# Half a batch of attention outputs turned on TensorE instead of by transposing transfers, with the order of commands written anew

## The chip, the cores and the metric

The kernel runs on one core of a Trainium2 chip. The metric is device time in microseconds (us) of one execution; the time of a version is the median over its runs. The profile is of one execution, and its span runs from that execution's first instruction to its last.

## What is computed

Masked attention over 4 batches of 8 heads (768 rows, 64 columns a head) is followed by a feed-forward layer that takes the largest of three products. "Retrieval" heads see every earlier row, the others only 4 sink rows and a window of 64.

```python
scores = scale * np.matmul(q, k.transpose(0, 1, 3, 2))
mask = np.where(retr[0, :, 0, 0, None, None], full_mask, stream_mask)
scores = np.where(mask[None, :, :, :], scores, -1000000000.0)
a = np.exp(scores - np.max(scores, axis=-1, keepdims=True))
a = a / (np.sum(a, axis=-1, keepdims=True) + 1e-09)
attn = np.matmul(a, v)                        # (4, 8, 768, 64)
x = attn.transpose(0, 2, 1, 3).reshape(4 * 768, 512)
h = np.maximum(np.maximum(x @ w1, x @ w2), x @ w3)   # (3072, 768)
out = h @ w_out                               # (3072, 512)
```

## The kernel before

The work is cut into batches (0 to 3) and halves of 384 rows. The order of all instructions is written out by hand: `PROGRAM` is a tuple of strings of short commands, and the loop at lines 843 to 846 calls a function for each, which issues its instructions there and then. Each engine works through its own in that order and waits where a tile isn't ready; so the table sets the order on every engine and on every queue of transfers. The commands that matter here, with their arguments (b batch, half, hp pair of heads):

- `load b quad` (line 248) loads keys and queries (tile kq) from POOL's queue, with a cast to 16 bits; `turn` (line 264) transposes them in 32 x 32 blocks on DVE into KQ. Batch 0 has its own path (`hl`, `cast`, `turnp`, `s0`, `k0`, `kx0`): two-head loads, casts, transposes on TensorE.
- `load_v b half s` (line 290) loads values from SP's queue in three transfers; `v` and `y` (lines 476, 512) cast them into the tiles va and vx. The last letter of a command names the engine that does it: d DVE, a ACT, p POOL, r DVE by a reduction. There are three buffers for the loaded values.
- `w 0` to `w 3` (line 391) load the three weights of the layer (w0t, w1t, w2t) and the output weight (woutt) from POOL's queue. `gs` (line 283) is a transfer of 4 bytes out of a weight tile on SP's queue: SP waits there until that weight has landed, and what follows on SP's queue comes later.
- `s b unit` (line 639) is a unit of scores on TensorE, followed by its exponentials on ACT (line 691) into tiles pt; there are two score tiles (st) in PSUM. `k` (line 696) multiplies pt by a mask, on POOL or DVE. `kx` gathers keys that the masks pick.
- `av b half hp` (line 703) multiplies probabilities with values for a pair of heads and divides by the sums on DVE (lines 722, 724). The result x has rows on the partitions and must be transposed into xT. With a trailing `D`, a transposing transfer on SP's queue does it (line 730). Without it, `x b half hp e` (line 736) does it: three TensorE transposes into a PSUM bank, then a copy by engine e (line 743).
- `f b half wi ni` (line 434) is one of 18 products of a half: four matmuls of 384 columns, then on ACT or DVE a cast (wi = 0) or on DVE a maximum (wi = 1, 2) into acc and hT. `o b half tb` (line 454) is an output block: six matmuls with woutt, a copy and a store on SP's queue.
- `idle n` (line 321) issues n matmuls on zeros, whose result nothing reads.

All TensorE results but the scores share four PSUM banks. In the table before, batch 0's half 0 is turned by TensorE, and in its half 1 pairs 0, 1 and 2 go by transfer and pair 3 by TensorE. All later halves go by transfer.

Of the kernel before, what the change touches and what calls it, by code (L numbers as in the profile page):

```python
# [96 lines left out]
    "s0 1 1 2, y 0 1 4:5:1 r r, gs 0, k0 0 3 2 d, f 0 0 0 5 a, kx 1 0 a, k0 2 1 0 p, turn 1 0 1 0",
    "k0 3 0 2 p, av 0 1 0 D, av 0 1 1 D, f 0 0 0 4 a, turn 1 1 0 0, turn 1 1 0 1, f 0 0 0 2 a",
    "f 0 0 0 0 a, f 0 0 1 0, load 2 0, f 0 0 1 5, turn 1 1 1 1, s0 1 2 2, k0 2 0 1 p",
    "turn 1 1 1 0, f 0 0 1 3, f 0 0 1 2, k0 2 0 0 p, y 0 1 5:8:2 r a, f 0 0 1 1, k0 3 1 2 p",  # L100
    "f 0 0 1 4, s 1 0, av 0 1 2 D, kx 1 1 p, k0 2 1 1 p, k0 2 3 1 p, av 0 1 3, f 0 0 2 0",
    "f 0 0 2 1, s 1 1, f 0 0 2 5, k 1 0 X 1 d, k 1 1 Y 0 p, f 0 0 2 2, turn 2 0 0 0, f 0 0 2 4",
    "turn 2 0 1 0, x 0 1 3 a, s 1 2, f 0 0 2 3, f 0 1 0 5 a, f 0 1 0 3 a, k 1 1 X 1 p",
    "turn 2 0 1 1, f 0 1 0 1 d, s 1 7, k 1 2 X 0 p, f 0 1 0 2 d, flags, load_v 1 0 s, v 1 0 0 d",
    "y 1 0 1:8:2 s a, v 1 0 1 a, gs 0, k 1 2 Y 0 d, y 1 0 4:5:1 s r, k 1 0 Y 0 p, f 0 1 0 0 d",
    "w 3, v 1 0 2 d, f 0 1 1 2, s 1 3, f 0 1 2 2, f 0 1 1 1, load_v 1 1 s, k 1 3 Y 0 p, f 0 1 1 3",
    "f 0 1 2 3, y 1 0 4:5:1 r a, y 1 0 1:8:2 r a, gs 0, f 0 1 0 4 d, s 1 5, k 1 0 X 0 d",
    "k 1 1 X 0 p, load_v 2 0 s, y 2 0 1:8:2 s a, f 0 1 1 5, f 0 1 2 5, y 1 1 1:8:2 r r",
    "k 1 7 X 1 p, y 1 1 4:5:1 r r, f 0 1 1 4, k 1 5 X 1 p, av 1 0 0 D, s 1 6, load 2 1",
    "av 1 0 1 D, v 1 1 2 d, f 0 1 1 0, v 1 0 3 a, f 0 1 2 0, f 0 1 2 1, k 1 2 X 1 p, av 1 0 2 D",  # L110
    "av 1 0 3 D, s 1 4, k 1 4 X 1 p, k 1 4 Y 0 p, f 0 1 2 4, v 1 1 3 p, o 0 0 0 a, o 0 0 1 a",
    "k 1 3 X 1 p, o 0 1 1 a, k 1 7 Y 1 d, turn 2 1 0 1, turn 2 1 1 1, k 1 4 X 0 p, v 1 1 1 p",
    "turn 2 1 0 0, turn 2 0 0 1, v 1 1 0 p, load_v 3 0 s, v 2 0 0 a, o 0 0 2 a, guess",
    "turn 2 1 1 0, f 1 0 0 1 a, f 1 0 0 0 a, f 1 0 1 0, f 1 0 0 5 d, k 1 7 X 0 p, v 2 0 1 p",
    "f 1 0 0 4 d, s 2 0, k 1 3 X 0 p, f 1 0 2 0, k 1 7 Y 0 d, load 3 0, k 1 6 X 0 p, f 1 0 1 4",
    "k 1 5 Y 0 d, v 2 0 2 a, kx 2 0 d, kx 2 1 a, f 1 0 2 4, f 1 0 1 1, k 1 5 X 0 d, f 1 0 0 3 a",
    "f 1 0 1 5, f 1 0 1 3, k 1 6 Y 0 p, av 1 1 3 D, av 1 1 1 D, s 2 1, k 2 1 Y 0 p, av 1 1 0 D",
    "y 2 0 1:8:2 r a, f 1 0 2 3, k 2 0 Y 0 p, gp 1 2, f 1 0 2 1, y 2 0 4:5:1 s a, av 1 1 2 D",
    "k 2 1 X 0 p, y 2 0 4:5:1 r a, v 3 0 0 p, s 2 4, f 1 0 2 5, f 1 0 0 2 d, load 3 1",
    "y 3 0 4:5:1 r d, v 2 0 3 a, f 1 0 1 2, f 1 0 2 2, s 2 2, k 2 2 X 0 d, f 1 1 0 0 d",  # L120
    "k 2 1 X 1 p, k 2 0 X 1 p, f 1 1 0 4 a, f 1 1 1 0, y 3 0 1:8:2 s a, k 2 2 X 1 d, turn 3 0 0 0",
    "y 3 0 1:8:2 r p, f 1 1 0 5 d, load_v 3 1 s, s 2 7, f 1 1 0 2 d, k 2 0 X 0 p, f 1 1 0 1 a",
    "o 0 1 0 d, f 1 1 1 1, av 2 0 0 D, k 2 4 Y 0 d, f 1 1 1 2, f 1 1 1 5, load_v 2 1 s",
    "k 2 4 X 1 d, k 2 7 Y 1 d, f 1 1 1 4, k 2 7 X 0 d, o 1 0 2 d, s 2 3, k 2 3 X 1 p",
    "turn 3 0 1 0, gs 0, k 2 2 Y 0 d, f 1 1 0 3 a, o 0 1 2 a, av 2 0 1 D, s 2 6, y 2 1 1:8:2 r a",
    "f 1 1 2 0, k 2 6 X 0 p, av 2 0 3 D, f 1 1 1 3, k 2 7 Y 0 d, s 2 5, k 2 6 Y 0 d, av 2 0 2 D",
    "f 1 1 2 4, f 1 1 2 3, f 1 1 2 5, turn 3 1 0 1, k 2 3 X 0 p, y 3 0 4:5:1 s a, o 1 0 1 a",
    "k 2 5 X 1 p, turn 3 0 1 1, turn 3 1 1 1, k 2 3 Y 0 p, v 3 1 0 d, v 2 1 2 a, o 1 0 0 a",
    "k 2 7 X 1 p, f 1 1 2 2, f 2 0 0 0 a, f 1 1 2 1, f 2 0 1 0, k 2 4 X 0 d, f 2 0 2 0",
    "f 2 0 0 1 a, turn 3 1 1 0, f 2 0 0 2 d, f 2 0 1 2, y 2 1 4:5:1 r p, v 3 0 3 p, v 3 1 2 a",  # L130
    "v 2 1 0 a, turn 3 1 0 0, f 2 0 0 4 a, f 2 0 1 4, v 3 1 1 p, turn 3 0 0 1, v 2 1 1 p",
    "kx 3 0 d, f 2 0 0 3 d, y 3 1 1:8:2 r d, k 2 5 Y 0 d, f 2 0 1 3, f 2 0 2 3, o 1 1 0 a, s 3 1",
# [909 lines left out]
```

## Time and profile before

| what | value |
|---|---|
| median of 3 runs | 190.68 us |
| all runs | 189.65, 190.68, 196.97 us |
| span of the profiled execution | 195.2 us |
| TensorE (PE) busy | 180.9 us, 93% of the span |
| DVE, ACT, POOL busy | 145.0, 98.8, 81.8 us |
| mean granted TensorE clock | 0.983 |

The profile gives the profiled execution's span and no other time of its own; the span lies 4.5 us above the median and 1.8 us below the slowest run. PE is TensorE's matmuls, DVE is VectorE, ACT is ScalarE, POOL is GpSimd, SP is the engine that only issues transfers; a q behind an engine's name (SPq) is its queue. L437 is line 437 of the kernel before. A row of a timeline gives start, duration, engine, line, what was written and read, and a count, with idle time and what ended it in brackets. A row of the windows gives, for a stretch of the span, each engine's busy time with its instructions, then the granted clock, the share of time that the transfer engines were busy (over 1 where packets wait) and GB/s.

### The profile page before, as it was taken

To read this page: it belongs to the slowest core of one execution; us is meant where nothing else is said; L and a number is where in the kernel's file an instruction comes from. 1 tells how busy PE (TensorE), PEld (TensorE's weight loads), DVE (VectorE), ACT (ScalarE), POOL (GpSimd) and SP (SyncE) were. 2 spreads that over 40 slices of the span, in tenths; PEclk is the share of its full clock that TensorE was granted. 3 is DMA by queue.
4 is the path that set the end of the run, shared out by engine and by line. 5 is a ranking of instruction groups with operands and counts; after the bars stand their busy time and mean duration, and the time that the engine had idled before them with its cause. 6 is when DMAs were issued, how large, how long until landed. Compare 5 with 4: busy or idle time off the path is not lost.

```text
span 195.2 us, 4739 instructions
## 1 busy us (share of the span) xinstructions
PE 180.9 (93%) x1854; PEld 106.1 (54%) x1854; DVE 145.0 (74%) x308; ACT 98.8 (51%) x158; POOL 81.8 (42%) x140
## 2 busy tenths in 40 slices
PE   7896899998994899999999999999999999999990
PEld 2443646664562445675556565755665566565550
DVE  3758999987997393879897989857794689465541
ACT  3598797377944534679529532775434400211110
POOL 7595978819682296039705600332612500000000
PEclk9999999999999589999999999999999999999999
DMA  5999999999999647935969310241033012401413
GB/s 177 329 325 267 207 213 207 116 164 189 160 187 227 97 133 158 242 99 108 210 167 241 93 58 0 77 114 57 0 66 129 0 57 59 134 0 54 161 54 116
DMA packets 44248, 26.59 MB, mean 136 GB/s; under 512 B 31038, under 2 KB 39742, under 8 KB 44222
## 3 DMA queue, kind: packets, MB, share of 16 engines
q1 hardware_dynamic: 38798, 17.54, 36.8%
q0 software_dynamic: 4192, 7.87, 23.8%
q10 hardware_dynamic: 1232, 0.85, 1.4%
q8 instruction: 15, 0.25, 0.5%
q14 instruction: 11, 0.09, 0.1%
HBM read 25.17 MB, written 6.29 MB: 161 GB/s over the span
## 4 chain that ended last, share of the span: by engine, by line
PE 66%; DMA 12%; DVE 11%; SPq 5%; issue 2%; ACT 1%; ACTq 0%; DVEq 0%
PE yy L437 34%; PE yy L462 15%; DMA vs<-in_v_dram 8%; PE oacc L717 6%; PE st L674 5%; DMA qs<-in_q_dram 4%; SPq L302 4%; DVE KQ L272 4%; PE yst L437 3%; DVE x L724 2%; DVE acc L449 1%; PE yst L462 1%; DVE KQ L241 1%; SPq L283 1%; DVE vx L800 1%
## 5 line engine op out<-in xcount | busy, mean ns | idle before, releaser
L377 POOL TENSOR_TENSOR pt<-pt,kb 128x512 f16<-128x512 f16 (+5 forms) x53 | 48.3, 931 | 67.4 <-ACT pt L691 55.5
L691 ACT ACTIVATE pt<-st 128x1024 f16<-128x1024 f32 (+2 forms) x51 | 43.5, 908 | 24.6 <-PE st L674 24.2
L437 PE MATMUL yy<-xT,w2t 128*128 128x384 f16 x184 | 36.8, 330 | 0.0
L437 PE MATMUL yy<-xT,w0t 128*128 128x384 f16 x180 | 34.9, 326 | 0.6 <-DMA xT<-x 0.6
L437 PE MATMUL yy<-xT,w1t 128*128 128x384 f16 x176 | 34.4, 326 | 0.1
L462 PE MATMUL yy<-woutt,hT 128*128 128x512 f16 (+1 forms) x138 | 32.8, 384 | 0.0
L449 DVE TENSOR_TENSOR hT<-yy,acc 128x384 f16<-128x384 f32 x46 | 25.2, 555 | 6.8 <-PE yy L437 5.1
L449 DVE TENSOR_TENSOR acc<-yy,acc 128x384 f16<-128x384 f32 x44 | 24.0, 555 | 7.9 <-PE yy L437 4.0
L272 DVE STREAM_TRANSPOSE KQ<-kq 128x384 f32<-128x384 f32 x24 | 25.4, 1134 | 0.4 <-DMA kq<-in_q_dram 0.4
L437 PEld LDWEIGHTS <-w0t 128*128 128x128 f16 x192 | 18.1, 98 | 13.5 <-issue 1.7
L445 ACT CAST acc<-yy 128x384 f16<-128x384 f32 x27 | 12.9, 489 | 23.3 <-PE yy L437 21.2
L437 PEld LDWEIGHTS <-w1t 128*128 128x128 f16 x192 | 17.9, 98 | 12.3 <-issue 1.0
L437 PEld LDWEIGHTS <-w2t 128*128 128x128 f16 x192 | 17.8, 98 | 12.3 <-issue 0.9
L462 PEld LDWEIGHTS <-hT 128*128 128x128 f16 x150 | 14.8, 101 | 16.5 <-issue 2.0
L717 PE MATMUL oacc<-va,pt 128*128 128x65 f16 x392 | 19.1, 195 | 4.4 <-ACT va L478 3.5
L717 PEld LDWEIGHTS <-pt 128*128 128x128 f16 x472 | 17.6, 98 | 8.3 <-issue 4.4
L471 ACT COPY ot<-yy 128x512 f32<-128x512 f32 (+1 forms) x14 | 7.9, 566 | 23.6 <-PE yy L462 20.9
L724 DVE TENSOR_TENSOR x<-oacc,sums 128x384 f16<-128x384 f32 x32 | 17.8, 557 | 1.1
L629 ACT ACTIVATE pt<-st 128x1024 f16<-128x1024 f32 (+5 forms) x22 | 15.5, 760 | 3.1 <-PE st L608 2.9
L674 PE MATMUL st<-KQ 32*128 32x128 f16 (+2 forms) x342 | 15.3, 263 | 0.0
L377 DVE TENSOR_TENSOR pt<-pt,kb 128x256 f16<-128x256 f16 (+4 forms) x31 | 11.7, 383 | 1.8 <-ACT pt L691 1.7
L445 DVE CAST acc<-yy 128x384 f16<-128x384 f32 x18 | 10.0, 557 | 3.8 <-PE yy L437 3.3
(117 smaller groups left out, 187.6 us busy)
## 6 DMA issues: line engine op xcount, KB each, us to landing
out_dram<-ot SPq DMA_DIRECT2D x23, 256.0 KB, 2.2
vs<-in_v_dram SPq DMA_DIRECT2D x18, 256.0 KB, 6.0
ks<-in_k_dram SPq DMA_DIRECT2D x8, 192.0 KB, 5.1
kq<-in_k_dram POOLq DMA_DIRECT2D x3, 384.0 KB, 8.1
kq<-in_q_dram POOLq DMA_DIRECT2D x3, 384.0 KB, 9.2
kq<-in_k_dram POOLq DMA_DIRECT2D x3, 288.0 KB, 7.9
kq<-in_q_dram POOLq DMA_DIRECT2D x3, 288.0 KB, 10.0
qs<-in_q_dram ACTq DMA_DIRECT2D x4, 192.0 KB, 4.8
```

Of the source, the lines that this page charges most:

```text
L272: nc.vector.transpose(out=dst.rearrange("c (p j) -> c j p", j=n)[:, j0:j1], in_=src.rearrange("c (j i) -> c j i", i=R),)
L377: engine.tensor_tensor(out=x, in0=x, in1=of_blocks(kb, pattern, rows), op=ALU.mult)
L437: nc.tensor.matmul(yy[:, 0:HALF], w_t[wi][:, ks, ni * P : (ni + 1) * P], xT[b, half, ks].rearrange("p a t -> p (a t)"), start=(ks == 0), s ...
L445: op(out=acc[b, half, ni], in_=yy[:, 0:HALF])
L449: nc.vector.tensor_tensor(out=acc[b, half, ni] if wi == 1 else hT[b, half, ni], in0=yy[:, 0:HALF], in1=acc[b, half, ni], op=ALU.max,)
L462: nc.tensor.matmul(yo[:, 0:n], hT[b, half, ns][:, tb * P : (tb + 1) * P], woutt[:, ns, c : c + n], start=(ns == 0), stop=(ns == NNB - 1),)
L471: op(out=ot[:, c : c + n], in_=yo[:, 0:n])
L629: nc.scalar.activation(out=pts[0, half, hp, u][:, r0:r1, c0:c1], in_=sts[hp][:, r0:r1, c0:c1], func=AF.Exp, scale=sc,)
L674: nc.tensor.matmul(sts["XY"[g // 2]][:, g % 2, c0 : c0 + n * P], KQ[rows, 0, ki * P : (ki + 1) * P] if kind == "p" else kx[b % 2][quad][ro ...
L691: nc.scalar.activation(out=pts[b, s, xy][:, r0:r1, c0:c1], in_=st[:, r0:r1, c0:c1], func=AF.Exp, scale=sc,)
L717: nc.tensor.matmul(o[:, i, r, 0 : D + 1], at[b, h, kind, ki, qi], vv[:, 0 : D + 1], start=(n == 0), stop=(n == len(todo) - 1), skip_group_ ...
L724: nc.vector.tensor_tensor(out=x, in0=o[:, :, :, 0:D], in1=rc.unsqueeze(3).to_broadcast([P, HB, 2, D]), op=ALU.mult,)
```

## The change

Only `PROGRAM` differs. `av 0 1 0`, `av 0 1 1` and `av 0 1 2` lose their `D`, and `x 0 1 0 d`, `x 0 1 1 a` and `x 0 1 2 a` are added; so three transfers go, and nine transposes, one copy on DVE and two on ACT come. Two of the `idle` commands are new with 2 matmuls each and one with 1: 18 such matmuls stand where 13 stood. Many other commands stand in another place, through the whole table, one goes to another engine (the cast of the queries of batch 0, half 1, pair 3, from DVE to POOL), and there are three more `gs 0`. Two of the places as lines of the table:

```diff
-    "s0 1 1 2, y 0 1 4:5:1 r r, gs 0, k0 0 3 2 d, f 0 0 0 5 a, kx 1 0 a, k0 2 1 0 p, turn 1 0 1 0",
-    "k0 3 0 2 p, av 0 1 0 D, av 0 1 1 D, f 0 0 0 4 a, turn 1 1 0 0, turn 1 1 0 1, f 0 0 0 2 a",
+    "av 0 1 0, av 0 1 1, f 0 0 0 5 a, w 2, k0 3 0 2 p, kx 1 0 a, k0 2 1 0 p, f 0 0 0 0 a",
+    "turn 1 0 1 0, turn 1 1 1 0, f 0 0 0 4 a, f 0 0 0 2 a, turn 1 1 0 1, turn 1 1 1 1",
+    "turn 1 1 0 0, x 0 1 1 a, s0 1 2 2, f 0 0 1 0, k0 3 1 2 p, k0 2 1 1 p, f 0 0 1 3",
```

Three places in the queues follow. Rows are instructions in an engine's order: line, operation, tile written <- tile read, shape, count. The lines of the changed kernel are four higher.

SP's queue, from the gate on w1t to the first transposing transfers of batch 1, before:

```order
L283 DMA gates<-w1t 1x2x1
L283 DMA gates<-w0t 1x2x1
L730 DMA_TRANSPOSE xT_685<-x 128x3x128
L730 DMA_TRANSPOSE xT_712<-x 128x3x128
L730 DMA_TRANSPOSE xT_828<-x 128x3x128
L302 DMA vs<-in_v_dram 128x8x64 x3
L283 DMA gates<-w0t 1x2x1
L302 DMA vs<-in_v_dram 128x8x64 x3
L283 DMA gates<-w0t 1x2x1
L302 DMA vs<-in_v_dram 128x8x64 x3
L730 DMA_TRANSPOSE xT_1207<-x 128x3x128
```

and now:

```order
L287 DMA gates<-w1t 1x2x1
L287 DMA gates<-w0t 1x2x1 x4
L306 DMA vs<-in_v_dram 128x8x64 x9
L734 DMA_TRANSPOSE xT_1254<-x 128x3x128
L734 DMA_TRANSPOSE xT_1278<-x 128x3x128
L287 DMA gates<-w0t 1x2x1 x2
```

The three transfers are gone, the gates between the loads of values stand ahead of them, and the nine loads follow each other. Their order also changes: before (batch 1, half 0), (1, 1), (2, 0); now (1, 0), (2, 0), (1, 1).

ACT around its first use of batch 2's values (the cast into vx_153; vx_154 is batch 1's), before:

```order
L691 ACTIVATE pt<-st 128x1024 x2
L524 CAST vx_154<-vs 64x2x64
L524 CAST vx_154<-vs 64x4x2x64
L691 ACTIVATE pt<-st 128x2x256
L691 ACTIVATE pt<-st 128x256
L691 ACTIVATE pt<-st 128x1024
L526 CAST vx_153<-vs 64x16x64
L691 ACTIVATE pt<-st 128x512
L691 ACTIVATE pt<-st 128x1024
```

and now:

```order
L530 CAST vx_154<-vs 64x16x64
L449 CAST acc<-yy 128x384 x2
L695 ACTIVATE pt<-st 128x512
L695 ACTIVATE pt<-st 128x1024 x3
L530 CAST vx_153<-vs 64x16x64
L695 ACTIVATE pt<-st 128x2x256
L695 ACTIVATE pt<-st 128x256
L695 ACTIVATE pt<-st 128x1024
```

The cast into vx_153 stood behind the exponentials of the unit `s 1 5` (the rows 2x256, 256 and 1024); now it stands ahead of them.

POOL around the loads of woutt and of batch 2's second quad of keys and queries, before:

```order
L766 CAST flagged<-both 1x2
L377 TENSOR_TENSOR pt<-pt,kb 128x2x2x128
L393 DMA woutt<-in_moe_w_out_dram 128x6x512
L377 TENSOR_TENSOR pt<-pt,kb 128x2x128
L377 TENSOR_TENSOR pt<-pt,kb 128x384
L377 TENSOR_TENSOR pt<-pt,kb 128x128
L377 TENSOR_TENSOR pt<-pt,kb 128x256
L257 DMA kq<-in_k_dram 32x1536
L257 DMA kq<-in_k_dram 96x1536
```

and now:

```order
L770 CAST flagged<-both 1x2
L574 COPY kx_158<-KQ 128x4x128
L579 COPY kx_158<-KQ 128x4x8
L381 TENSOR_TENSOR pt<-pt,kb 128x512
L397 DMA woutt<-in_moe_w_out_dram 128x6x512
L381 TENSOR_TENSOR pt<-pt,kb 128x2x384
L381 TENSOR_TENSOR pt<-pt,kb 128x512
L261 DMA kq<-in_k_dram 32x1536
L261 DMA kq<-in_k_dram 96x1536
```

woutt stood behind a comparison of flags (the small row `flagged`) and a late mask of `s 1 0`, with masks of `s 1 1` and `s 1 2` done before; now it stands directly behind the first mask of `s 1 1`. The load of kq stood behind masks of `s 1 7` and `s 1 5`, and now behind a mask of `s 1 2`. Further up on POOL, `w 1` stood ahead of the load of batch 1's second quad; now it stands behind it and behind the first mask of batch 0's half 1.

129 rows, old and new, of the table PROGRAM are left out of this document.

## The prediction

> **What bounds the kernel now.** I read the busy time by stretches of the span first, then the list of waits, then the timelines of the engines around the one long wait. A row of the first view gives, for a stretch, the busy time of PE, its weight loads, DVE, ACT and POOL, then the granted clock.
>
> ```profile
> span 195.2 us, 4739 instructions
> 6.00:26.00 20.00, 16.16 (x204) 9.61 (x204) 15.78 (x38) 16.74 (x29) 15.29 (x33) 1.00 1.11 275
> 26.00:60.00 34.00, 32.83 (x391) 19.67 (x388) 31.24 (x60) 22.42 (x37) 24.89 (x43) 1.00 1.17 179
> 60.00:70.00 10.00, 6.50 (x56) 3.56 (x54) 5.73 (x12) 4.88 (x7) 2.87 (x4) 0.66 0.80 139
> 70.00:190.00 120.00, 120.00 (x1191) 71.07 (x1190) 89.18 (x191) 52.91 (x84) 34.68 (x49) 1.00 0.39 99
> 190.00:195.20 5.20, 0.70 (x8) 0.36 (x6) 0.56 (x1) 0.27 (x1) 0.00 (x0) 1.00 0.32 112
> ```
>
> From 70 to 190 us PE has no idle time at all: there the time is the sum of the matmuls, and a new order can only lose. Idle time stands at the start (3.84 us of 6 to 26), a little from 26 to 60 (1.17 us), and in one hole between 60 and 70 us (3.50 us), after which PE runs at a lower clock. The hole is read from ACT, PE and the chain of work that ended last:
>
> ```profile
> 51.10 10.15 DMA vs<-in_v_dram
> 55.04 1.79 ACT L691 ACTIVATE pt<-st 128x512 f16<-128x512 f32 x3 [1.19 <-PE st L674]
> 61.28 1.04 ACT L526 CAST vx<-vs 64x1024 f16<-64x1024 f32 x1 [4.45 <-DMA vs<-in_v_dram]
> 62.23 1.49 ACT L691 ACTIVATE pt<-st 128x512 f16<-128x512 f32 x2
> 60.48 0.19 PE L717 MATMUL oacc<-va,pt 128*128 128x65 f16 x1
> 64.17 0.65 PE L717 MATMUL oacc<-va,pt 128*128 128x65 f16 x9 [3.50 <-ACT va L478]
> ```
>
> ACT stands at its cast of batch 2's values from 56.83 us, because that load lands at 51.10 + 10.15 = 61.25 us. Everything behind it on ACT waits too, exponentials and a value cast, so PE runs out of work at 60.67 us and resumes 2.9 us after the landing. The clock row says 0.66 over 10 us; with full speed elsewhere and half speed in the slow part, that is 6.8 us at half speed, 3.4 us of work lost. The hole cost 3.5 + 3.4 = 6.9 us.
>
> Why the load was late is on SP's queue and POOL's:
>
> ```profile
> 29.70 0.72 SPq L283 DMA_DIRECT2D gates<-w1t  x1
> 30.52 0.56 SPq L283 DMA_DIRECT2D gates<-w0t  x1
> 31.51 9.27 SPq L730 DMA_TRANSPOSE xT<-x  x3
> 40.84 4.35 SPq L302 DMA_DIRECT2D vs<-in_v_dram  x3
> 45.23 1.19 SPq L283 DMA_DIRECT2D gates<-w0t  x1
> 46.52 3.85 SPq L302 DMA_DIRECT2D vs<-in_v_dram  x3
> 50.41 0.59 SPq L283 DMA_DIRECT2D gates<-w0t  x1
> 51.10 6.18 SPq L302 DMA_DIRECT2D vs<-in_v_dram  x3
> 50.53 0.92 POOL L393 DMA_DIRECT2D woutt<-in_moe_w_out_dram  x1
> 56.32 1.08 POOL L257 DMA_DIRECT2D kq<-in_k_dram  x2
> woutt<-in_moe_w_out_dram POOLq DMA_DIRECT2D x1, 768.0 KB, 10.3
> ```
>
> SP is held by the three transposing transfers until 40.84 us, so batch 2's load (the last three) is issued from 51.10 us, beside woutt (50.53 to 50.53 + 10.3 = 60.8 us), and lands as woutt does.
>
> **How the profiled time stands to the runs.** The span is 195.2 us, the runs 189.65, 190.68 and 196.97. Without the hole the span is 195.2 - 6.9 = 188.3. I read the two fast runs as executions in which that load won its race and the slow one as like the profile. The time outside the span is then 189.65 - 188.3 = 1.4 us from below and 196.97 - 195.2 = 1.8 us from above; I take 1.4, and 0 as the lowest, since nothing shows it directly. So a change that only removes the hole lands at the median, not 7 us under it.
>
> **The change part by part.** The turning itself:
>
> ```profile
> 25.42 0.17 PE tr L740 x3
> L743 ACT COPY xT<-tr x2: 479/480/480, 23.8 to 43.4; 128x384 f16<-128x384 f16 x2
> L743 DVE COPY xT<-tr x3: 345/346/393, 23.3 to 25.8; 128x384 f16<-128x384 f16 x3
> L730 SPq DMA_TRANSPOSE xT<-x x27: 1177/1206/5747, 31.5 to 165.5; - x27
> PE yy L437 <- DMA xT<-x: 0.6, 1, 0.6
> 95.07 1.29 PE yy L462 x6
> ```
>
> - Nine transposes: 3 x 0.17 = +0.5 us on PE, on the path since PE is full from 26 us.
> - Three copies: 2 x 0.48 us on ACT, 0.35 on DVE. ACT is busy 22.42 of 34 us, and the four products between a transpose and its use cover a copy; 0, at most 0.5 for a bank freed late. The cast given to POOL takes one cast off DVE in the start, about as much as the DVE copy adds.
> - The transfers gone: PE's one wait for xT goes, -0.6 us. Their 1.2 us each on SP (5.75 the longest) mattered only through what stood behind them.
> - Five more dummy matmuls of 512 columns: at 1.29 / 6 = 0.215 us, 1.1 us. All but the last stand ahead of 26 us, where PE has 3.84 us idle; 0, and 1.1 if that cover is gone.
> - Moves in the start: between -2 and +1 us of its 3.84, since the first products wait for weights; I take 0.
>
> The weights are the next term. Their issues and landings:
>
> ```profile
> 14.44 0.77 POOL L398 DMA_DIRECT2D w0t<-in_moe_w_dram  x1
> 18.59 0.75 POOL L398 DMA_DIRECT2D w1t<-in_moe_w_dram  x1
> 28.27 0.83 POOL L398 DMA_DIRECT2D w2t<-in_moe_w_dram  x1
> w0t<-in_moe_w_dram POOLq DMA_DIRECT2D x1, 768.0 KB, 11.4
> w1t<-in_moe_w_dram POOLq DMA_DIRECT2D x1, 768.0 KB, 11.1
> w2t<-in_moe_w_dram POOLq DMA_DIRECT2D x1, 768.0 KB, 9.4
> L437 PE MATMUL yy<-xT,w1t x176: 323/326/337, 33.0 to 175.9; 128*128 128x384 f16 x176
> 77.59 4.66 PE yy L437 x28
> ```
>
> They land at 25.8, 29.7 and 37.7 us. Between w1t and w2t the queue carried a load of kq: 8.0 us for two loads, 4.0 each. Now kq goes ahead of w1t, so w1t lands near 29.7 + 4.0 = 33.7 us; w2t keeps its place. PE's first product with w1t began at 33.0 us. Now a score unit and a transpose that came later stand ahead of it (about 0.5 us), and one score unit has moved the other way, so PE is there between 32.5 and 33.5. It waits up to 1.2 us, but has then done work that it did later before: +0.3 us net, between 0 and 3 (if kq takes longer or the start gains 2 us that w1t eats).
>
> Then the values, beside two rows of ACT, the exponentials of `s 1 1` and `s 1 3`:
>
> ```profile
> 41.16 1.94 ACT L691 ACTIVATE pt<-st 128x1024 f16<-128x1024 f32 x2 [1.08 <-PE st L674]
> 51.09 1.92 ACT L691 ACTIVATE pt<-st 128x1024 f16<-128x1024 f32 x2
> ```
>
> SP's gate opens with w1t, at 33.7 us; five gates of 0.56 to 1.19 us bring SP to about 37 us, 4 us sooner than 40.84. Batch 2's load is now second: issued from 37 + 4.35 = 41.4 us, not 51.10. But its reader moved as well. The cast into vx no longer waits behind the exponentials of `s 1 5`, so ACT asks for it when those of `s 1 3` end, near 53 us, not at 56.83. And POOL issues woutt behind the first mask of `s 1 1` (41.16 + half of 1.94 + about 1 us of mask, 43 us) and the kq load two masks later, near 47, not at 50.53 and 56.32. So the load again runs beside both. How long it takes then is bounded by the load of values with the most and the median time from issue to landing in that stretch:
>
> ```profile
> DMA to landing us min/median/max: 5.6/6.7/15.7
> ```
>
> The third issue near 45 us plus 6.7 is 52 us; 41.4 + 15.7 is 57 us. PE has seven products (4.66 / 7 = 0.67 us each) and a score unit left when the scores of `s 1 3` end near 51, hence work to about 56, and ACT needs 2 us after a landing. PE waits for landing - 54: 0 at 52 us, 3 at 57. I take 55 us, between, so +1.0 us, and from 0 to 3.5.
>
> Does such a wait cost clock as well? The trace's one gap of that size, 3.50 us, did; the 3.84 us of the start, in many pieces, fall where the clock reads 1.00. [...]
>
> The sum: 195.2 - 3.5 - 3.4 + 0.5 - 0.6 + 0.3 + 1.0 + 1.4 = 190.9 us. The later rearrangement (70 to 190 us) counts 0, because PE is full there before and its work is the same.
>
> **The rivals.**
>
> - *The hole comes back whole (slower).* Place: ACT's cast into vx_153. In favour: woutt and kq now both start inside the load's time, and ACT asks 4 us sooner; against: the load starts 9.7 us sooner. It decides from a landing at 57.5 us: PE waits 3.5 us and loses 3.4 to the clock: 189.6 + 0.3 + 6.9 = 196.8 us. (189.6 is the sum without the w1t and value terms.) [...]
> - *Nothing moves.* The transfers were hidden, and the hole belongs to some executions only. In favour: two of three runs lie 6 to 7 us under the third, and just one wait in the list is for xT, 0.6 us. Without late weights and late values: 189.6 us.
> - *w1t is very late.* POOL issues it about 6 us later than 18.59. In favour: it now stands behind a mask that needs exponentials; against: the queue has a backlog until then. 3 us of waiting: 189.6 + 3.0 = 192.6 us.
> - *The start gains (faster).* Half of the 3.84 us idle goes, and no later load takes it back: 189.6 - 2.0 = 187.6; with the time outside the span at 0.5, 186.7 us. In favour: loads and casts are placed with more work between; against: w0t lands at 25.8 us whatever PE does.
>
> **How the numbers follow.** Short wait for values (my forecast, 188.5 to 193.5 us): 0.49. Hole back: 0.22. Nothing moves: 0.13. Faster start: 0.10. w1t very late: 0.06. The spread of the runs lets a measurement tell about 2% from no change, so the bounds are 186.9 and 194.5 us. Faster by over 2%: 0.10, the start's gain. Slower: the hole, plus 0.03 for w1t waits long enough to cost clock, 0.25. Within: 0.65. The predicted time is 190.9 us. The range reaches down to 188.0, which leaves out the faster start, and up to 196.5, which leaves out the upper half of the returned hole: 188.0 to 196.5.
>
> **What would show it.** Right: no wait of PE for xT in batch 0; SP's loads of values begin near 37 us; PE's first w1t product at 33 to 34 us behind a short wait; ACT waiting for vs at its second cast, near 53 us, and a gap on PE under 3 us with the clock row at 1.00 from 50 to 70; PE full from 70 us on. [...]

## The result and the profile after

The changed kernel takes 196.88 us (median of 14 runs, 192.66 to 204.49), the kernel before, beside it on the same chips, 193.56 us (14 runs, 189.65 to 200.75). The ratio is 1.014, with a 95% interval of 1.0093 to 1.0187: 1.4% slower. The median lies above the predicted range. Executions of either kernel differ by 11 to 12 us; the ratio leaves the long ones out, and the profiled execution of the changed kernel, 200.81 us, is a long one, so its profile holds one loss that the ratio doesn't. Seven of the changed kernel's executions took 192.66 to 194.78 us and seven 198.97 to 204.49, and the median lies between the two groups. Before's own median is 2.9 us higher over the 14 runs than over the three that the prediction had (190.68).

First the same stretches as in the prediction, of the changed kernel, the long stretch cut in two:

```profile
span 199.1 us, 4762 instructions
6.00:26.00 20.00, 12.89 (x161) 8.02 (x160) 13.00 (x31) 13.28 (x24) 9.75 (x23) 0.94 1.01 258
26.00:60.00 34.00, 32.14 (x376) 19.51 (x379) 27.51 (x52) 24.40 (x38) 29.01 (x52) 0.94 0.98 166
60.00:70.00 10.00, 9.86 (x130) 6.13 (x124) 9.71 (x23) 7.52 (x13) 4.53 (x6) 1.00 0.80 171
70.00:100.00 30.00, 27.57 (x315) 16.21 (x314) 24.32 (x46) 17.34 (x27) 16.10 (x24) 1.00 0.79 162
100.00:190.00 90.00, 90.00 (x860) 52.59 (x858) 66.27 (x148) 34.96 (x56) 18.00 (x25) 1.00 0.27 77
```

Three things have changed. The hole of 60 to 70 us is gone: PE works 9.86 of 10 us at clock 1.00 (6.50 at 0.66 before). The start has a new hole: 12.89 of 20 us (16.16 before). And from 70 to 100 us, where PE was full, it now idles 30 - 27.57 = 2.4 us. After 100 us it is full as before.

The new hole in the start, on PE, POOL and SP's queue (line numbers of the changed kernel are four higher than before's):

```profile
27.17 1.44 PE L509 MATMUL vb<-vn,every 128*128 128x512 f16 x3 [5.90 <-POOL vn L501]
25.53 1.59 POOL L501 CAST vn<-vs 128x768 f16<-128x768 f32 x2 [6.57 <-DMA vs<-in_v_dram]
27.07 1.03 POOL L261 DMA_DIRECT2D kq<-in_k_dram  x2
30.32 0.83 POOL L402 DMA_DIRECT2D w1t<-in_moe_w_dram  x1
12.35 0.47 SPq L299 DMA_DIRECT2D vs<-in_v_dram  x1
```

PE stands 5.90 us because batch 0's second half of values, issued at 12.35 us, lands only at 25.5 us. POOL stands at their cast too, so the loads behind it on its queue, kq and w1t, are issued 8 and 12 us later than before.

The values of batch 2, the middle of the forecast, on SP, ACT and POOL:

```profile
38.40 0.72 SPq L287 DMA_DIRECT2D gates<-w1t  x1
41.65 19.45 SPq L306 DMA_DIRECT2D vs<-in_v_dram  x7
59.11 1.04 ACT L530 CAST vx<-vs 64x1024 f16<-64x1024 f32 x1
65.41 0.50 POOL L482 CAST va<-vs 128x384 f16<-128x384 f32 x1 [3.53 <-DMA vs<-in_v_dram]
```

ACT finds the values there at 59.11 us and waits for nothing; POOL waits 3.53 us for others, and PE for none of it. (This execution reaches that point late, through the hole in the start; but in `old_then_new` below, with before's start, ACT comes to this cast at 53.30 us, near the predicted 53, and doesn't wait either.) What PE waited for between 60 and 100 us, in the changed kernel:

```profile
PE yy L441 <- DVE hT L453: 1.2, 1, 1.2
PE yy L441 <- ACT acc L449: 0.6, 1, 0.6
PE yy L441 <- DMA xT<-x: 0.5, 1, 0.5
```

Together 2.3 of the 2.4 us. These are new: a product of the layer that waits for a bank of PSUM (hT, acc) or for batch 1's turned outputs (xT).

### The profile page after: what moved, and what is told of

Read it like the earlier page. It is cut to its first block, busy times and chain, and to the rows that moved or that the text cites. A ratio compares the mean times of both kernels' runs of the same rounds, so it can differ in the third digit from the quotient of the medians.

```text
span 199.1 us, 4762 instructions
## 1 busy us (share of the span) xinstructions
PE 181.4 (91%) x1868; PEld 106.3 (53%) x1868; DVE 145.2 (73%) x308; ACT 99.8 (50%) x160; POOL 82.0 (41%) x141
## 4 chain that ended last, share of the span: by engine, by line
PE 71%; DMA 11%; DVE 9%; POOL 2%; issue 2%; SPq 2%; ACT 0%; DVEq 0%; POOLq 0%
PE yy L441 40%; PE yy L466 13%; DMA vs<-in_v_dram 7%; PE oacc L721 7%; PE st L678 6%; PE yst L441 3%; DMA ks<-in_k_dram 3%; DVE KQ L276 2%; DVE x L728 1%; DVE hT L453 1%; POOL vn L501 1%; DVE pt L381 1%; DMA xT<-x 1%; PE yst L466 1%; DVE acc L453 1%
## 5 line engine op out<-in xcount | busy, mean ns | idle before, releaser
L381 POOL TENSOR_TENSOR pt<-pt,kb 128x512 f16<-128x512 f16 (+5 forms) x53 | 47.7, 923 | 60.6 <-ACT pt L695 48.9
L441 PE MATMUL yy<-xT,w2t 128*128 128x384 f16 x184 | 36.2, 327 | 0.0
L441 PE MATMUL yy<-xT,w0t 128*128 128x384 f16 x176 | 33.7, 327 | 2.4 <-DVE hT L453 1.2
L441 PE MATMUL yy<-xT,w1t 128*128 128x384 f16 x180 | 35.2, 327 | 0.1
L466 PE MATMUL yy<-woutt,hT 128*128 128x512 f16 (+1 forms) x138 | 31.8, 373 | 0.0
L453 DVE TENSOR_TENSOR acc<-yy,acc 128x384 f16<-128x384 f32 x45 | 24.6, 556 | 9.0 <-PE yy L441 6.2
L453 DVE TENSOR_TENSOR hT<-yy,acc 128x384 f16<-128x384 f32 x46 | 25.5, 556 | 5.3 <-PE yy L441 3.1
L276 DVE STREAM_TRANSPOSE KQ<-kq 128x384 f32<-128x384 f32 x24 | 25.8, 1128 | 0.0
L441 PEld LDWEIGHTS <-w1t 128*128 128x128 f16 x192 | 17.9, 98 | 12.9 <-issue 0.7
L449 ACT CAST acc<-yy 128x384 f16<-128x384 f32 x26 | 12.1, 480 | 22.2 <-PE yy L441 22.1
L466 PEld LDWEIGHTS <-hT 128*128 128x128 f16 x150 | 14.0, 98 | 14.8 <-DVE hT L453 0.2
L475 ACT COPY ot<-yy 128x512 f32<-128x512 f32 (+1 forms) x15 | 8.5, 565 | 25.0 <-PE yy L466 21.7
L678 PEld LDWEIGHTS <-KQ 32*128 32x128 f16 x342 | 8.9, 92 | 7.7 <-issue 7.1
```

The source lines that it names most:

```text
L276: nc.vector.transpose(out=dst.rearrange("c (p j) -> c j p", j=n)[:, j0:j1], in_=src.rearrange("c (j i) -> c j i", i=R),)
L381: engine.tensor_tensor(out=x, in0=x, in1=of_blocks(kb, pattern, rows), op=ALU.mult)
L441: nc.tensor.matmul(yy[:, 0:HALF], w_t[wi][:, ks, ni * P : (ni + 1) * P], xT[b, half, ks].rearrange("p a t -> p (a t)"), start=(ks == 0), s ...
L449: op(out=acc[b, half, ni], in_=yy[:, 0:HALF])
L453: nc.vector.tensor_tensor(out=acc[b, half, ni] if wi == 1 else hT[b, half, ni], in0=yy[:, 0:HALF], in1=acc[b, half, ni], op=ALU.max,)
L466: nc.tensor.matmul(yo[:, 0:n], hT[b, half, ns][:, tb * P : (tb + 1) * P], woutt[:, ns, c : c + n], start=(ns == 0), stop=(ns == NNB - 1),)
```

## The experiments

My theory after this profile was that the order after the first product costs, since the waits at 70 to 100 us lie there. The rivals: the turning itself, the start, and an order that costs through something that no wait shows. Each group of runs had the kernel before beside it on the same chip; ratios are to that. Line numbers in the runs are those of before, or one higher.

**Start, rest and turning apart.** Four runs: the changed kernel again; the start of before with the rest of the new table; the new start with the rest of before, transfers included; and before with only the turning changed, which is

```diff
- av 0 1 0 D, av 0 1 1 D, ... f 0 0 0 0 a, f 0 0 1 0 ... av 0 1 2 D
+ av 0 1 0,   av 0 1 1,   ... f 0 0 0 0 a, x 0 1 1 a, f 0 0 1 0 ... av 0 1 2
- f 0 0 2 1, s 1 1, f 0 0 2 5, k 1 0 X 1 d
+ f 0 0 2 1, x 0 1 2 a, s 1 1, f 0 0 2 5, x 0 1 0 d, k 1 0 X 1 d
```

`again`:

> The changed kernel once more, beside the kernel before on the same chip. Theory A (the start: SP issues batch 0's second half of values about 1 us later, they land late behind POOL's loads, POOL's cast of them waits, and with it the loads of batch 1's keys and of w1t that stand behind that cast): 2 to 3 us over before, with a wait of PE for vn of 1 us or more and PE full again from 35 to 70 us. Rival B (the rest of the order, from the first product on, and the nine transposes cost it): 2 to 3 us over before too, but with a wait for vn under 0.5 us and the idle time of PE after 35 us.

`start_old`:

> The commands ahead of the first product in the order of the kernel before, all that follows as in the changed kernel (the five new dummy matmuls left out). Theory A: the loss goes, within 1 us of before, and no wait for vn. Rival B: still 2 to 3 us over before.

`start_new`:

> The commands ahead of the first product in the order of the changed kernel, all that follows as in the kernel before, the three transposing transfers included. Theory A: 2 to 3 us over before, with the wait for vn. Rival B: within 1 us of before.

`turn_only`:

> The kernel before, with the three transfers replaced by TensorE transposes and copies and no other command moved; SP then reaches batch 1's values as soon as its gates open, near 31 us. Theory A: within 1 us of before. Rival B, in the form that the transposes and their copies cost: 1 us or more over before. If the hole at batch 2's values in the profile of before came from the transfers, that hole is gone here.

| run | median us (lowest to highest) | ratio to before, 95% |
|---|---|---|
| before | 192.23 (191.21 to 196.74) | |
| again | 199.39 (192.81 to 205.4) | |
| start_old | 197.42 (196.89 to 197.73) | 1.0294 (1.0253 to 1.0335) |
| start_new | 190.42 (190.1 to 203.51) | 0.9926 (0.9885 to 0.9967) |
| turn_only | 191.13 (190.71 to 191.48) | 0.9968 (0.9929 to 1.0008) |

Turning costs nothing, and the four runs of `turn_only` lie within 0.8 us. `again` repeats both losses in its profile: PE waits 5.5 us for vn, and 1.2 us for hT between 60 and 100 us. The new start gains 0.7% in three of four executions; the fourth took 203.51 us. The new rest stays slow with the old start. But `start_old` says too much: I had left one cast of the start (pair 1 3) on POOL, as in the new table. In its profile POOL stands there, and PE behind it:

```profile
15.65 0.51 POOL L221 CAST qn<-qs 128x384 f16<-128x384 f32 x1 [3.46 <-DMA qs<-in_q_dram]
18.06 0.50 PE L239 MATMUL tr<-ident,kn 128*128 128x128 f16 x3 [2.98 <-POOL kn L221]
```

So its 2.9% is partly my mixture's. The next runs have the old start whole and leave out the three added `gs 0` too.

**The rest in two halves.** Three mixtures with the turning on TensorE: the new order from the first product on; the new order only from there to the output products at 78 us; and only from these on. A fourth run is `start_new` with the turning of `turn_only` added.

`old_then_new`:

> The order of before up to the first product, casts and all, and from there the order of after, outputs of batch 0's half 1 turned by TensorE. If the order after the start is what costs (my theory now), the time is that of the run that only turns, 191.1, plus the 2.4 us that TensorE was idle between 70 and 100 us in after: 193.5, and TensorE's busy time between 65 and 100 us is about 32.5 of 35 us. If the loss of after lies in its start alone, this is 191.1 and TensorE is full there. The 197.4 of the earlier mixture of old start and new rest would come back only if the rest itself costs 6 us; I expect it not to, since that mixture also had one cast of the start moved to POOL, which waited 3.5 us.

`new_to_78`:

> As the run before it in this list, but the order of after is followed only up to the three output products o 0 0 1, o 0 0 0, o 0 1 1 (about 78 us), and from there that of before. If there are two separate losses, one at the wait for batch 1's turned outputs at 73 us (1.1 us) and one at 90 to 100 us (1.3 us) from the later order, this is 191.1 + 1.1 = 192.2. If DVE's backlog of before 70 us makes both, it is 193.5. If the loss is all in the later order, 191.1.

`new_from_78`:

> The other half: the order of before, only turned by TensorE, up to and with o 0 1 1, and from there the order of after. Two separate losses: 191.1 + 1.3 = 192.4. Backlog made before 70 us: 191.1. All in the later order: 193.5.

`new_start_turned`:

> The start of after, the rest of before, and the three outputs turned by TensorE: the run that had after's start with before's rest (190.4), with nothing changed but the turning. If turning is free once its products stand beside full work, 190.4, at most 0.5 us either way. If the turning products cost their time on TensorE (three times four products of about 0.06 us and the waits for their copies), 191. If the start's late load of values comes in the profiled execution, TensorE has only 4 to 5 us of work between 20 and 30 us and that execution is near 200.

| run | median us (lowest to highest) | ratio to before, 95% |
|---|---|---|
| before | 191.25 (189.81 to 200.42) | |
| old_then_new | 195.0 (194.56 to 195.43) | 1.0198 (1.013 to 1.0267) |
| new_to_78 | 192.37 (192.02 to 193.15) | 1.0072 (1.0036 to 1.0108) |
| new_from_78 | 193.08 (192.6 to 194.4) | 1.012 (1.004 to 1.0201) |
| new_start_turned | 193.76 (191.25 to 199.63) | |

Against `turn_only` (0.9968) the whole new rest costs 2.3 points, and the halves 1.0 and 1.5: two separate losses that add up within the intervals, each larger than I expected (0.6 and 0.7). In `old_then_new` PE idles 2.2 of the 40 us from 60 to 100, about half of the 4.4 us by which the 2.3 points put it over `turn_only`. The rest isn't placed; that execution's clock also reads 0.86 from 20 to 30 us, where `turn_only` has 1.00. `new_start_turned` scatters as the changed kernel does, and its two shorter executions, 191.25 and 191.32 us, show nothing of the new start's gain beside 191.25 for before.

**Two pieces, put back and put in.** The larger loss is a wait for hT near 88 us. In the new table a unit of scores and its two masks on DVE stand ahead of the products f 1 0 2 2 (before has the second mask further behind them), and a turn of keys on DVE stands earlier. `turn_late_hT` is `turn_only` with only this piece:

```diff
- av 1 1 2 D, k 2 1 X 0 p, ... f 1 0 2 2, s 2 2, k 2 2 X 0 d, ... k 2 2 X 1 d, turn 3 0 0 0
+ av 1 1 2 D, turn 3 0 0 0, k 2 1 X 0 p, ... s 2 2, k 2 2 X 0 d, k 2 2 X 1 d, f 1 0 2 2
```

`from_78_hT` is `new_from_78` with the piece taken out. `three_mended` is `old_then_new` without this piece, and with two others moved: SP's two gates, to behind all four of batch 1's transfers, with the output product o 0 0 2 put back; and the mask k0 0 1 2. The mask was no test: `old_then_new` already has it ahead of the first product, and here it only moves directly up to that product, behind commands for the values. `start_mended` is `new_start_turned` with the cast of pair 0 2 put back.

`turn_late_hT`:

> The same piece done alone, the other way round: the order of before, outputs turned by TensorE, and only f 1 0 2 2 moved behind s 2 2 and its two masks on DVE, and the turn 3 0 0 0 moved ahead to just behind the outputs av 1 1 2. If the piece is the cost, 1.0 to 1.3 us above the run that only turns (0.3% under before): about 0.3% above before, and TensorE waits 1 us for hT near 85 us. If it needs the rest of after's order to hurt, no change: 0.3% under before, no such wait.

`from_78_hT`:

> The order of before up to 78 us and that of after from there, with two commands put back: the products f 1 0 2 2 ahead of the scores s 2 2 and their masks, and the turn of batch 3's keys 3 0 0 0 behind these masks. If DVE's queue in front of that one hT is what made the half from 78 us slow, the wait of TensorE for hT (1.3 us at 88 us) goes and the time falls from 1.0% above before to about 0.4% above or less (192.1 beside a before of 191.3). If the wait only moves to the next product behind the same DVE work, the time stays at +1.2%.

`three_mended`:

> The run with before's start and after's order from the first product (2.0% above before), with three pieces put back: the mask k0 0 1 2 ahead of the first product (TensorE waited 0.9 us for it at 30 us, 0.3 in the order of before), the two gates of SP behind batch 1's four transposing transfers with the product o 0 0 2 ahead of the next hidden products (waits of 0.3 and 0.6 us at 68 us), and the hT piece of the other runs (1.3 us at 90 us). The waits add up to 2.8 us: if they add in the time too, 1.0198 - 0.0146 = 1.005 of before. If only the hT piece counts, 1.013. If the order loses by something that no wait shows, 1.02.

`start_mended`:

> After's start and before's rest, turned by TensorE (191.3 to 199.6 in four executions), with one command put back where before has it: the cast of pair (0,2), ahead of clear 0 and the first turned pair, so that SP's loads wait less for its buffer and the last load of values is issued near 11.4 us instead of 11.9 to 12.9. If the late issue is what lets POOL's loads hold up its last pieces (values landed at 19.4 us when issued at 11.6 and at 25.5 when issued at 12.4), every execution is 190 to 192. If the issue time has nothing to do with it, one or two in four are again 198 or more.

| run | median us (lowest to highest) | ratio to before, 95% |
|---|---|---|
| before | 192.31 (190.34 to 196.45) | |
| turn_late_hT | 194.09 (193.12 to 195.03) | 1.0125 (1.0014 to 1.0237) |
| from_78_hT | 193.39 (192.74 to 194.13) | 1.0109 (1.001 to 1.0208) |
| three_mended | 193.59 (192.89 to 198.42) | 1.0107 (1.006 to 1.0153) |
| start_mended | 194.66 (193.02 to 195.75) | 1.0181 (1.0077 to 1.0285) |

Put in alone, the piece costs 1.6 points of per cent, some 3 us, over `turn_only` (1.0125 against 0.9968; both intervals are about half a point to a point wide either way), more than the 1.0 to 1.3 us that I expected. DVE and PE of `turn_late_hT`:

```profile
81.85 0.19 DVE L722 RECIPROCAL sums<-oacc 128x6 f32<-128x6 f32 x1
82.54 1.13 DVE L272 STREAM_TRANSPOSE KQ<-kq 128x384 f32<-128x384 f32 x1
84.55 1.14 DVE L524 CAST vx<-vs 64x128 f16<-64x128 f32 x1
86.41 2.72 DVE L377 TENSOR_TENSOR pt<-pt,kb 128x512 f16<-128x512 f16 x2
89.06 0.55 DVE L449 TENSOR_TENSOR hT<-yy,acc 128x384 f16<-128x384 f32 x1
89.65 0.81 PE L437 MATMUL yy<-xT,w0t 128*128 128x384 f16 x4 [1.66 <-DVE hT L449]
```

And DVE of the base, run once more (`turn_again`, below), around the same maximum into hT:

```profile
80.10 0.19 DVE L722 RECIPROCAL sums<-oacc 128x6 f32<-128x6 f32 x1
83.96 0.56 DVE L449 TENSOR_TENSOR acc<-yy,acc 128x384 f16<-128x384 f32 x1
84.63 0.56 DVE L449 TENSOR_TENSOR hT<-yy,acc 128x384 f16<-128x384 f32 x1
85.10 0.41 DVE L377 TENSOR_TENSOR pt<-pt,kb 128x512 f16<-128x512 f16 x1
87.30 1.12 DVE L272 STREAM_TRANSPOSE KQ<-kq 128x384 f32<-128x384 f32 x1
```

In the base hT follows the maximum before it at once, and masks and key turn come after. With the piece, DVE does the key turn (1.13) and both masks (2.72) first. hT comes 4.4 us later, of which 1.75 is this execution's being later as a whole (the reciprocals in the first rows, 81.85 and 80.10); 2.7 us are the piece's, and PE has no free bank for 1.66 of them. So hT had about 1 us to spare in the base.

The 1.75 us are not the piece's. They come from the start, which both kernels share, where this execution ran at a lower clock; the base first, then `turn_late_hT`:

```profile
20.00:30.00 10.00, 8.95 (x121) 5.29 (x117) 9.34 (x24) 9.13 (x14) 8.74 (x14) 1.00 1.14 211
20.00:30.00 10.00, 9.87 (x111) 6.48 (x112) 8.34 (x22) 7.50 (x10) 7.70 (x12) 0.70 1.14 210
```

Behind that stretch PE's first product begins at 28.38 us instead of 26.75, already 1.63 us late. So the piece's own price in the profile is the wait, 1.66 us, and the 3 us of the ratio may hold some of the clock's.

Taking the piece out of the new order does not give the time back. In `from_78_hT` the wait for hT is gone, but the next product waits behind the same DVE work:

```profile
85.88 1.89 DVE L377 TENSOR_TENSOR pt<-pt,kb 128x512 f16<-128x512 f16 x2 [0.40 <-ACT pt L691]
87.69 1.12 DVE L272 STREAM_TRANSPOSE KQ<-kq 128x384 f32<-128x384 f32 x1
88.60 0.59 DVE L445 CAST acc<-yy 128x384 f16<-128x384 f32 x1
89.25 0.81 PE L437 MATMUL yy<-xT,w0t 128*128 128x384 f16 x4 [1.08 <-DVE acc L445]
```

That was the second branch of its expectation. `three_mended` gains 0.9 points of the expected 1.5, and a wait of 1.1 us for xT at 85.7 us stands where the wait for hT was. `start_mended` is no better, with no execution under 193 and none above 196 us: the cast put back moved POOL's order, and PE waited 3.0 us for the late values all the same, issued at 11.62 us and there at 21.95.

**The half before 78 us, and the start.** Base again with five rounds; the mask alone moved; SP's gates and the output product alone moved; and the changed kernel with POOL's loads ahead of its casts of the late values:

```diff
mask_late       - k0 0 1 2 d, f 0 0 0 3 a, ... k0 0 3 2 d
                + f 0 0 0 3 a, ... k0 0 3 2 d, k0 0 1 2 d
gates_between   - v 1 0 1 a, gs 0, ... y 1 0 1:8:2 r a, gs 0, ... av 1 0 1 D, ... av 1 0 2 D ... o 0 0 2 a ... f 1 0 0 1 a, f 1 0 0 0 a
                + v 1 0 1 a, ... y 1 0 1:8:2 r a, ... av 1 0 1 D, ... gs 0, f 0 1 2 0, gs 0, ... av 1 0 2 D ... f 1 0 0 1 a, f 1 0 0 0 a, o 0 0 2 a
loads_first     - vc 1 4 4 p, ... vc 1 0 4 p, ... load 1 1, ... w 1
                + w 1, load 1 1, vc 1 4 4 p, ... vc 1 0 4 p
```

`turn_again`:

> The run that only turns the three outputs by TensorE, once more, as the base of the next three. If turning alone is free it is again 190.7 to 191.5, 0 to 0.5% under before; if the first four executions were lucky, it scatters like before (190 to 196).

`mask_late`:

> The run that only turns, with one command moved as in after: the mask k0 0 1 2 on DVE behind the mask k0 0 3 2 instead of ahead of the first product. In the runs with after's order TensorE waited 0.9 to 1.0 us at 30 us for a mask of DVE, in the order of before 0.3. If this mask is the one, 0.6 us above the base; but putting it back in the run with three pieces mended left the wait at 1.0 us, so it may be another of DVE's commands there, and then there is no change.

`gates_between`:

> The run that only turns, with SP's two gates moved as in after between batch 1's transposing transfers, and the output product o 0 0 2 behind the next hidden products. If these make the waits of 0.3 and 0.6 us for xT and the bank after it, 0.9 us above the base and the wait shows near 66 us. If the transfers have slack in the order of before, no change.

`loads_first`:

> After whole, with POOL's issues of w1t and of batch 1's second keys put ahead of its two casts of the late values, as in before. Mine: half of after's executions are 198 and more since POOL stands 6 us at these casts and the loads behind it start late; with the loads ahead all executions are under 197 and the median is near the fast executions of after, 1.4% above before. Rival: the values themselves land late for TensorE (it needs them turned), so the loads ahead of them change nothing or take more of the DMA from them: half the executions stay at 198 or more.

| run | median us (lowest to highest) | ratio to before, 95% |
|---|---|---|
| before | 193.74 (190.25 to 203.27) | |
| turn_again | 190.97 (189.78 to 191.58) | 0.9934 (0.9893 to 0.9975) |
| mask_late | 190.96 (190.19 to 191.82) | 0.9977 (0.994 to 1.0015) |
| gates_between | 193.03 (192.16 to 194.14) | 1.0038 (0.9996 to 1.008) |
| loads_first | 201.03 (195.35 to 203.71) | |

The mask is not it. The gates and the product are: 2.1 us between the medians of the same call, and the twelve runs of each don't overlap. SP's queue in the base, in `gates_between`, and PE there:

```profile
58.71 5.75 SPq L730 DMA_TRANSPOSE xT<-x  x4
64.55 2.31 SPq L472 DMA_DIRECT2D out_dram<-ot  x3
```

```profile
58.73 3.76 SPq L730 DMA_TRANSPOSE xT<-x  x2
62.55 1.23 SPq L283 DMA_DIRECT2D gates<-w0t  x2
63.88 3.19 SPq L730 DMA_TRANSPOSE xT<-x  x2
```

```profile
67.00 0.32 PE L437 MATMUL yy<-xT,w0t 128*128 128x384 f16 x1 [0.77 <-DMA xT<-x]
68.22 0.97 PE L437 MATMUL yy<-xT,w0t 128*128 128x384 f16 x5 [0.90 <-DMA xT<-x]
```

The gates open at once (w0t landed long before; in before it had landed by 25.8 us) and still take 1.23 us of SP's queue. The last transfer leaves it at 63.88 + 3.19 = 67.07 us instead of 58.71 + 5.75 = 64.46, and the products that need the turned outputs wait 0.77 + 0.90 us.

`loads_first` went against me: four of its six executions were still above 199 us, and the other two above 195. In its profile POOL issues w1t at 18.48 us and both kq loads, and casts the values at 21.26 us; PE then has 7.41 us of work between 20 and 30 us. That execution, 195.59 us, is one of the two shorter ones: its values took 9.6 us to land (11.68 to 21.26), and PE waited 2.2 us for them. So moving POOL's loads ahead of the casts does not cure the long executions, as the rival had it. What makes the four long ones isn't seen, since none of them was profiled.

**Do the two pieces make the whole?** `gates_only` is `gates_between` with o 0 0 2 left in its place; `both_pieces` is `turn_only` with `gates_between` and `turn_late_hT` together.

`gates_only`:

> The run that only turns, with only SP's two gates moved between batch 1's transposing transfers; the output product o 0 0 2 stays where before has it. With the product moved too it was 1.0% above the base, TensorE waiting 1.7 us for xT at 67 us. The gates take 1.2 us of SP's queue, o 0 0 2 1.3 us of TensorE: if the cover of the product is what counts, this is at most 0.3% above the base and the wait is under 0.5 us; if the gates alone do it, 1.0% again.

`both_pieces`:

> The run that only turns, with the two pieces of after's order that cost when put in alone: gates and o 0 0 2 (+1.0%) and the queue of DVE ahead of one hT (+1.6%). If these two are what makes the whole new order after the first product slow (2.0 to 2.3% above the base), 1.020 to 1.026 times the base, which is 194.8 to 196 us. If one hides the other (TensorE late at 67 us gives DVE time to catch up by 85 us), 1.016, 194 us.

Beside before at 192.68 us (189.66 to 201.67), `gates_only` took 192.83 us (191.61 to 194.28; ratio 1.0076, 1.0013 to 1.0139) and `both_pieces` 194.66 us (194.47 to 195.23; 1.0142, 1.0075 to 1.0208). The gates alone already cost what gates and product cost within the intervals, though the one profiled execution, the third fastest of the ten, shows a single wait of 0.54 us between 60 and 100 us; how much the product adds stays open. The two pieces together show PE's work in `turn_again` first, then in `both_pieces`, over 60 to 70, 70 to 80 and 80 to 90 us:

```profile
60.00:70.00 10.00, 9.97 (x83) 5.44 (x80) 9.09 (x16) 5.55 (x9) 7.53 (x13) 1.00 1.06 208
70.00:80.00 10.00, 10.00 (x155) 6.97 (x157) 7.96 (x21) 5.84 (x9) 1.86 (x3) 1.00 0.80 162
80.00:90.00 10.00, 10.00 (x118) 5.77 (x112) 8.51 (x16) 8.45 (x13) 9.67 (x13) 1.00 0.70 139
```

```profile
60.00:70.00 10.00, 8.29 (x68) 4.31 (x68) 8.34 (x13) 5.06 (x8) 7.68 (x13) 1.00 0.78 157
70.00:80.00 10.00, 10.00 (x141) 6.78 (x140) 7.09 (x18) 4.57 (x8) 1.37 (x2) 1.00 0.96 195
80.00:90.00 10.00, 8.19 (x108) 5.04 (x105) 9.46 (x15) 8.53 (x12) 8.47 (x11) 1.00 0.60 116
```

Two holes of 1.7 and 1.8 us, 3.5 us, where the base has none; the medians differ by 194.66 - 190.97 = 3.7 us. The whole new rest, `old_then_new`, was at 195.0, on another chip; by the ratios it is 1.7 to 2.1 points for the two pieces (1.0142 against 0.9968 and 0.9934) and 2.3 to 2.6 for the whole. So six moved commands are enough for most of what the whole new order costs, and they don't hide one another. They are not all that costs: `three_mended`, with these six undone or moved out of the way, still lies 1.4 to 1.7 points over the run that only turns.

The best of the versions is the smallest change: `turn_only`, at 190.97 us, is 0.7% under before (0.9934, 0.9893 to 0.9975 in the five rounds), and its sixteen executions lie between 189.78 and 191.58 us, where before scatters up to 203. Three executions of `start_new` were shorter than its median (190.1 to 190.47), but the fourth was the one of 203.51.

## Why the prediction was wrong

Two of its steps failed. The first explains why the shorter executions of the changed kernel are slower than before; the second is seen in the two long ones that were profiled, and without the long ones the median would have stayed inside the range.

- **The step that failed: "The later rearrangement (70 to 190 us) counts 0, because PE is full there before and its work is the same."** With before's start, the new order after the first product costs 2.0% of before, 4.4 us over the run that only turns (1.0198 against 0.9968). PE was full before only because DVE freed each bank and SP delivered each xT in time, and I never looked at how much in time: at 85 us it is about 1 us, and at 67 us less than the 2.6 us by which the gates made the last transfer later. I wrote that there "a new order can only lose", and then priced the loss at nothing without reading a single wait against the new order. Which other moves cost, beside the six of `both_pieces`, stays open.
- **Moves in the start, "between -2 and +1 us of its 3.84, since the first products wait for weights; I take 0": failed for the long executions.** In both profiled executions of the changed kernel, 200.81 and 201.04 us, the second half of batch 0's values lands only near 25.5 us, PE waits 5.9 and 5.5 us for it, and they lie 6 to 8 us above the shorter ones (192.66 to 194.78). No rival held this; I looked for late weights in the start and passed over the values. Issued at 11.6 to 12.9 us, that load took 7.8 us in the profile of `start_new` and about 13 in those of the changed kernel. What decides it stays open: neither an earlier cast (`start_mended`) nor POOL's loads ahead (`loads_first`) cured it. Where the load comes in time, the new start gains 0.7%, 1.4 us, in `start_new`, inside the bounds, and nothing in `new_start_turned`. What the five dummy matmuls do wasn't tried apart.
- **The hole at 60 us goes: right.** Turning alone removes it (9.97 of 10 us at clock 1.00, and none of sixteen executions above 191.58 us), as the prediction reasoned through SP's queue: batch 2's load is issued from 44.29 us in `turn_only`, not from 51.10. The wait of +1.0 us that was to take its place did not come; that term is 0. That such a wait would cost no clock besides, as the sum has it, was the author's assumption: no run shows the term. In before the clock fell only with the wait of 3.50 us, to 0.50, and in `both_pieces` waits of up to 1.7 us left it at 1.00.
- **The hole's price, 6.9 us: 0.6 too much.** In the profile of before the clock reads 0.50 from 63.0 to 69.8 us, and PE stood idle until 64.17; that part of the slow stretch was counted twice. The four matmuls of 384 columns at 65.84 us took 1.46 us there, as long as eight at 58.91 us, so the slow part cost (69.8 - 64.17) / 2 = 2.8 us, not 3.4, and the span without the hole is 188.9 us. `turn_only` and `turn_again` have 189.0 and 189.3.
- **Turning costs 0.5 us, and a wait for xT of 0.6 goes: right in kind.** The net of all that turning does is -0.3 and -0.7% in two measurements. PE's list of waits shows none for the copies.
- **Late w1t, +0.3 us: borne out in kind.** With the new start and values in time, SP's gate on w1t opens at 32.97 us in `start_new` (the prediction had 33.7), and PE waits 0.8 us for w1t there and 0.6 in `new_start_turned`. In the profiled execution of the changed kernel PE's first product with it begins at 40.55 us, without a wait, since the start's hole had moved everything.
- **Time outside the span, 1.4 us: too small by 0.3.** 200.81 - 199.1 = 1.7 us for the profiled run, and 192.66 less its own span, 190.9, is 1.8 us for the fastest.

Put together from measured ratios, 1.0198 for turning and the new order and 0.9926 for the new start, the changed kernel comes to 1.012 of before, inside the measured interval (1.0093 to 1.0187). That the second factor rests on three executions, and didn't show in `new_start_turned`, makes this agreement weaker than it looks.

The clock followed long waits, but not only them. In before it reads 1.00 from 62.0 to 62.5 us and 0.50 from 63.0 to 69.8, with PE out of work from 60.67 to 64.17 us. In the changed kernel it reads 1.00 from 21 to 23 us and 0.50 from 24 to 30, with PE out of work from 21.27 to 27.17 us. The waits of up to 1.7 us in `both_pieces` left it at 1.00 in the rows of 60 to 90 us. `turn_late_hT` has no long wait ahead of its slow stretch: its clock reads 0.92 from 15 to 20 us and 0.70 from 20 to 30, and apart from 1.3 us at its first dummy matmuls and the 1.66 us at 89.65 us no wait in PE's list is over 0.9 us. Before has waits of 0.70 and 0.65 us between 17 and 20 us, and its clock reads 1.00 from 15 to 26 us. From 15 to 20 us PE was busy for 3.47 of 5 us in `turn_late_hT` and for 3.27 in before. So with about the same work the clock fell in one execution and not in the other, and what decides it isn't shown.

## What to carry to other kernels

A stretch where TensorE is 100% busy says that its work is the bound there, not that its order is free: before a reordering is priced at nothing, read how long ahead of its use each bank is freed and each transfer lands, and price what is put in front of it on its own engine's queue. Here a wait on a condition long met still occupied its queue: two such gates in `gates_between` took 1.23 us of SP and, with transfers behind them that TensorE needed, about 2 us of the kernel. And try the core of a change by itself; here it was a small gain, and the moves around it were the loss.

## What was not expected of the hardware

- The same load of values (768 KB on SP's queue, issued between 11.6 and 12.9 us) landed after 7.8 us in `start_new` and after about 13 us in the changed kernel: POOL's casts, which wait for it, begin at 19.45 and at 25.53 us. 0.7 us in the issue goes with 6 us in the landing, but the issue time alone doesn't decide it: issued at 11.62 us it took 10.3 us (`start_mended`), and at 11.94 us 7.5 us (`new_start_turned`).
- A transfer of 4 bytes that waits for nothing took about 0.6 us of SP's queue (two in a row took 1.23 us in `gates_between`; the median of the nine on w0t in the changed kernel is 0.56 us), half of a transposing transfer's median of 1.2 us in before.
- One mask on DVE took up to 0.83 us in the base and 1.97 in `turn_late_hT` (the numbers behind the colon are minimum, median and maximum in ns); first the base:

```profile
L377 DVE TENSOR_TENSOR pt<-pt,kb x31: 214/335/832, 29.1 to 153.9; 128x256 f16<-128x256 f16 x11, 128x512 f16<-128x512 f16 x10, 128x128 f16<-128x128 f16 x6, 128x1024 f16<-128x1024 f16 x3
```

```profile
L377 DVE TENSOR_TENSOR pt<-pt,kb x31: 215/334/1968, 30.8 to 157.3; 128x256 f16<-128x256 f16 x11, 128x512 f16<-128x512 f16 x10, 128x128 f16<-128x128 f16 x6, 128x1024 f16<-128x1024 f16 x3
87.64 2.50 POOL L377 TENSOR_TENSOR pt<-pt,kb 128x512 f16<-128x512 f16 x2
```

  The long one, 87.16 to 89.13 us, ran for the most part beside POOL's masks of the last row. But in the base a mask of the same shape (86.56 us) took 0.82 us beside POOL's masks (85.88 us, 2.51 us for two), and no run here took POOL's masks away; so what made the long one longer isn't shown.
